# Two batches' attention masks moved to TensorE, and first loads spread over three queues

## The chip, the cores and the metric

The kernel runs on one core of one Trainium2 chip. The metric is the time of one execution in device microseconds (us). Before the change it is 325.88 us, the median of three runs (325.7 to 327.67).

A core has five engines that run their own instruction streams in order and wait for one another through semaphores: PE (TensorE, matrix products and transposes), DVE (VectorE), ACT (ScalarE), POOL (GpSimd) and SP (SyncE, which here only issues DMAs). DMAs can be issued from SP, ACT or POOL. Only those from POOL convert f32 to bf16 on the way in this kernel.

## The reference, cut to what matters

Two stages follow each other. A sparse attention over 8 batches of 8 heads, 576 positions and 64 dimensions; the first four heads see the last 32 positions ("local"), the other four see the earlier positions with the same remainder by 32 ("strided"). Then a feed-forward layer with an ELU.

```
scores = q @ k.T / sqrt(64)
mask_local   = (rel >= 0) & (rel < 32)
mask_strided = (rel >= 0) & (pos[None, :] % 32 == pos[:, None] % 32)
scores = where(masks, scores, -1e9)          # heads 0-3 local, 4-7 strided
attn = exp(scores - max); attn = attn / (sum(attn) + 1e-9)
x = (attn @ v) as [4608, 512]
h = x @ w_in                                 # [4608, 2048]
out = where(h > 0, h, exp(min(h, 0)) - 1) @ w_out
```

Inputs and output are f32.

## The kernel before, in words

**Attention.** A batch has four pairs of heads: two strided (`s0`, `s1`) and two local (`l0`, `l1`). For a strided pair the positions are sorted by remainder into five groups per head, of 126, 126, 108, 108 and 108 keys and queries, so that each group is one small block; the local pairs use six blocks of 128 keys by 96 queries per head. For each pair, PE transposes q and k (`t_q`, `t_k`, L361 strided and L375 local) into one PSUM bank, and ACT or DVE copies that to SBUF (L364, L378). `scores(u)` (L481) makes the scores of unit u = 0 or 1, half of the blocks each, in a pair of PSUM banks (`pair_a` or `pair_b`); ACT takes the exp into bf16 (L501); `mask(u)` (L506) multiplies the probabilities on DVE by a mask of zeros and ones (L516). There is no maximum subtracted. `av(u)` (L520) multiplies with v, which carries a column of ones, so that the sum of each row comes out too; DVE takes its reciprocal (`rden`, L543) and scales (L544) to `x_s` or `x_l`. `x_out` transposes that into `xT` (L571 strided, L584 local; copies L578, L580 and L588). `halo` (L421) copies the last 32 rows of each local v block to the next block; `v_in` (L414) copies the strided v from `v_raw` to `v_str`. From batch 3 on, other forms of the scores are used (L443), with the masks still on DVE.

**Feed-forward.** 4608 tokens are nine chunks of 512. For each chunk and each of 16 slices m of the hidden layer, PE adds four matmuls of 512 columns (L622), ACT takes the exp (L648), DVE forms min(e, 1) - 1 (L655) and the maximum with h (L657). In chunk 0, the slices in ON_SCALAR take another way: ACT does a Relu as well (L651) and DVE one instruction (L652). The output product is L667, copied by ACT (L671) and stored by SP.

**Order.** Each engine's order is written out by hand. OPENING (L45) lists the steps of batch 0, with fill matmuls on data that nobody reads (L712, `fill.n`) and the first twelve matmuls of chunk 0 (`moe.c`, for c the slice of xT); `S0`, `S1` are batch 1's strided pairs. After it, the attention of batch n+1 is put between the matmuls of chunk n by a table of starts and pitches (TIMES).

**Loads.** `load_strided` (L167) issues five DMAs for one tensor of a batch: one for each head (108 rows of 320 elements) and one for the remaining 18 rows. Batch 0's q goes over SP as f32 into `q_stage`, and is cast by ACT (first pair) and DVE (second pair) at L348. All else goes over POOL and is converted on the way, in this order: strided k, local q, local k, strided v, local v, then batch 1 mixed with `w_in` (L302 to L327). Ahead of them POOL makes the identity and the index ramps from which DVE builds the masks (L263 to L298).

Of the kernel before, what the change touches and what calls it, by code (L numbers as in the profile page):

```python
# [10 lines left out]
F32 = mybir.dt.float32  # L11
BF16 = mybir.dt.bfloat16
I32 = mybir.dt.int32
# [40 lines left out]
ON_SCALAR = (4, 7, 10, 13, 15)  # L54
# [4 lines left out]
def kernel(  # L59
# [74 lines left out]
    mask_w = consts.tile([128, 2 * 126 + 3 * 108], BF16, tag="mask_w")  # L134
    mask_s, mask_s3 = mask_w[:, 0:252], mask_w[:, 252:576]
# [27 lines left out]
    WHOLE = 3  # L163
    raw = {}
# [69 lines left out]
    def clear_nat(i, engine=nc.vector):  # L234

        for name in "kq":
            t = nat[name, "str"][i].rearrange("p (h x) -> p h x", h=4)
            engine.memset(t[96:128], 0.0)
# [6 lines left out]
    def clear_v(i, engine=nc.vector):  # L245
# [8 lines left out]
             for n in "q"}  # L254
    load_strided(0, "q", nc.sync)
# [14 lines left out]
    rel_i = p_k.tile([128, LB], I32, tag="rel_i")  # L270
    nc.gpsimd.iota(rel_i, pattern=[[1, LB]], base=32, channel_multiplier=-1)
# [3 lines left out]
    nc.tensor.transpose(key_ps[0:126, 0:126], key_q[0:126, :], identity[0:126, 0:126])  # L275
    diff = p_k.tile([128, 126], F32, tag="diff")
# [13 lines left out]
    rel = p_k.tile([128, LB], F32, tag="rel")  # L290
    above = p_k.tile([128, LB], F32, tag="above")
    nc.vector.tensor_copy(rel, rel_i)
# [37 lines left out]
    class Pair:  # L330
# [150 lines left out]
        def scores(self, u):  # L481
# [4 lines left out]
            blocks = self.blocks(u)  # L486
            for p, blk, bank, i, nk, nq in blocks:
                at, half = self.place(p, blk)
                d = slice(64 * half, 64 * half + 64)
                kind = "str" if self.strided else "loc"  # L490
                c = 0 if self.strided else LB * blk

                nc.tensor.matmul(sc[:, bank, i * nq:(i + 1) * nq],  # L493
                                 lhsT=kT[kind][self.b % 2][d, at, c:c + 128],
                                 rhs=qT[kind][self.b % 2][d, at, c:c + nq],
                                 start=True, stop=True)
# [6 lines left out]
            if self.b:  # L503
                self.mask(u)
# [45 lines left out]
        def step(self, what):  # L550
# [3 lines left out]
            elif what[1:].isdigit():  # L554
                {"s": self.scores, "m": self.mask, "a": self.av}[what[0]](int(what[1:]))
            else:
                getattr(self, {"x": "x_out"}.get(what, what))()
# [388 lines left out]
```

## Time and profile before

| | |
|---|---|
| median of 3 runs | 325.88 us |
| profiled execution | 327.16 us |
| its span | 325.3 us |
| PE busy | 301.5 us (93%) |
| DVE busy | 243.3 us (75%) |
| ACT busy | 177.8 us (55%) |
| POOL busy | 131.4 us (40%) |
| DMA q0 (POOL's): packets, MB | 67632, 18.10 |
| DMA q1 (SP's): packets, MB | 34469, 17.11 |

The profile shows one execution. Its span begins with the first instruction; all times within it are counted from there. Busy shares are means over the whole span, so they do not say which engine holds up which part. In rows of instructions "x" is the number of them, the first figures are start and length in us, and what stands in brackets is the idle time ahead and what ended it. PE lengths include a latency that neighbours overlap, so that rates are read from the distance of starts. A few per cent of the matmul records are missing (558 of 576 of the output product are there).

### The profile page before, as it was taken

The page shows a single profiled execution, that of the slowest core. Times are in us where ns is not written, and L with a number is a line of the kernel's source. Part 1 is how long each engine was busy: PE and PEld are TensorE (multiplying, and loading weights), DVE is VectorE, ACT ScalarE, POOL GpSimd, SP SyncE. Part 2 cuts the span into 40 slices and gives each one's busy share as a digit, 9 for nine tenths or more (in the row PEclk, how much of TensorE's full clock was granted, in tenths as well). Part 3 has the DMA queues.
Part 4 walks back from the last instruction along what each step waited for, and adds up shares of the span by engine and source line. Part 5 has one row for each costly group of instructions (what it writes and reads, how often), then busy time and mean ns, then how long its engine had stood idle before and what let it go on. Part 6 is the DMA issues. An engine that isn't in the chain of part 4 may idle for free.

```text
span 325.3 us, 6088 instructions
## 1 busy us (share of the span) xinstructions
PE 301.5 (93%) x2205; PEld 150.8 (46%) x2246; DVE 243.3 (75%) x539; ACT 177.8 (55%) x337; POOL 131.4 (40%) x208
## 2 busy tenths in 40 slices
PE   2697888999999999999999999999999999999992
PEld 1463544555544554444444454454445444444440
DVE  6576887787888788988798879887887666866600
ACT  3577885776455664555555655555565444434320
POOL 9579825958389368839823830000000000000000
PEclk9999999999999999999999999999999999999998
DMA  6999999999999999999988992920210001100012
GB/s 112 154 169 120 168 207 139 148 130 162 158 141 97 106 154 172 139 182 169 148 117 143 148 135 62 153 83 35 55 48 32 33 34 54 43 35 33 32 67 72
DMA packets 102138, 35.67 MB, mean 110 GB/s; under 512 B 79885, under 2 KB 97493, under 8 KB 102101
## 3 DMA queue, kind: packets, MB, share of 16 engines
q0 software_dynamic: 67632, 18.10, 64.6%
q1 hardware_dynamic: 34469, 17.11, 24.8%
q8 instruction: 19, 0.31, 0.4%
q14 instruction: 18, 0.15, 0.2%
HBM read 36.70 MB, written 9.44 MB: 142 GB/s over the span
## 4 chain that ended last, share of the span: by engine, by line
PE 86%; DVE 4%; DMA 3%; ACT 3%; issue 2%; POOL 2%; ACTq 0%; POOLq 0%
PE single L667 38%; PE half L622 28%; PE single L622 9%; PE single L535 3%; DMA k_loc<-in_k_dram 3%; PE pair_a L456 2%; PE single L375 2%; PE single L571 1%; ACT e_sb L648 1%; PE pair_a L493 1%; DVE g_sb L657 1%; POOL k_str L178 1%; DVE x_l L544 1%; DVE x_s L544 1%; DVE g_sb L652 1%
## 5 line engine op out<-in xcount | busy, mean ns | idle before, releaser
L667 PE MATMUL single<-w_out_sb,g_sb 128*128 128x512 bf16 x558 | 143.6, 379 | 1.4 <-DVE g_sb L657 0.4
L622 PE MATMUL half<-xT,w_in_sb 128*128 128x512 bf16 x419 | 110.3, 379 | 1.1 <-issue 0.3
L648 ACT ACTIVATE e_sb<-half 128x512 f32<-128x512 f32 x109 | 65.3, 599 | 68.7 <-PE half L622 62.4
L655 DVE TENSOR_SCALAR e_sb<-e_sb 128x512 bf16<-128x512 f32 x139 | 62.0, 446 | 36.5 <-ACT e_sb L648 35.4
L667 PEld LDWEIGHTS <-g_sb 128*128 128x128 bf16 x576 | 53.5, 98 | 59.6 <-DVE g_sb L657 1.2
L622 PEld LDWEIGHTS <-w_in_sb 128*128 128x128 bf16 x576 | 51.7, 98 | 55.2 <-issue 0.2
L657 DVE TENSOR_TENSOR g_sb<-e_sb,half 128x512 bf16<-128x512 bf16 x104 | 71.5, 688 | 3.6
L622 PE MATMUL single<-xT,w_in_sb 128*128 128x512 bf16 x136 | 36.0, 379 | 0.3 <-issue 0.2
L648 ACT ACTIVATE e_sb<-single 128x512 f32<-128x512 f32 x35 | 21.1, 602 | 21.6 <-PE single L622 19.6
L671 ACT COPY o_sb<-single 128x512 f32<-128x512 f32 x36 | 21.1, 586 | 17.7 <-PE single L667 16.5
L535 PEld LDWEIGHTS <-pr 128*128 128x128 bf16 (+3 forms) x352 | 20.9, 105 | 15.0 <-issue 1.1
L178 POOL DMA_DIRECT2D v_raw<-in_v_dram x32 | 19.9, 659 | 15.8 <-DVE v_str L414 15.7
L462 ACT ACTIVATE pr<-pair_a 126x936 bf16<-126x936 f32 (+1 forms) x20 | 19.2, 962 | 11.8 <-PE single L456 11.8
L657 DVE TENSOR_TENSOR g_sb<-e_sb,single 128x512 bf16<-128x512 bf16 x35 | 24.1, 688 | 1.2
L178 POOL DMA_DIRECT2D k_str<-in_k_dram x32 | 20.1, 647 | 7.6 <-issue 3.6
L178 POOL DMA_DIRECT2D q_str<-in_q_dram x28 | 17.6, 651 | 6.3 <-DMA w_out_sb<-in_moe_w_out_dram 2.0
L544 DVE TENSOR_TENSOR x_l<-single,rden 96x384 bf16<-96x384 f32 x32 | 17.7, 554 | 1.1
L501 ACT ACTIVATE pr<-pair_a 128x576 bf16<-128x576 f32 (+2 forms) x20 | 13.1, 653 | 6.9 <-PE pair_a L493 6.9
L544 DVE TENSOR_TENSOR x_s<-single,rden 126x256 bf16<-126x256 f32 (+1 forms) x32 | 15.7, 491 | 1.1
L543 DVE RECIPROCAL rden<-single 96x6 f32<-96x6 f32 (+2 forms) x64 | 11.9, 185 | 3.6 <-PE single L535 3.2
L201 POOL DMA_DIRECT2D q_loc<-in_q_dram x16 | 12.3, 794 | 3.2 <-DMA k_str<-in_k_dram 1.6
L182 POOL DMA_DIRECT2D k_str<-in_k_dram x8 | 4.8, 606 | 19.4 <-PE single L375 6.3
(114 smaller groups left out, 269.0 us busy)
## 6 DMA issues: line engine op xcount, KB each, us to landing
out_dram<-o_sb SPq DMA_DIRECT2D x36, 256.0 KB, 2.2
v_loc<-in_v_dram POOLq DMA_DIRECT2D x8, 288.0 KB, 9.7
k_str<-in_k_dram POOLq DMA_DIRECT2D x32, 67.5 KB, 4.6
v_raw<-in_v_dram POOLq DMA_DIRECT2D x32, 67.5 KB, 4.4
w_in_sb<-in_moe_w_in_dram POOLq DMA_DIRECT2D x4, 512.0 KB, 9.2
w_out_sb<-in_moe_w_out_dram POOLq DMA_DIRECT2D x4, 512.0 KB, 16.7
q_str<-in_q_dram POOLq DMA_DIRECT2D x28, 67.5 KB, 6.9
q_loc<-in_q_dram POOLq DMA_DIRECT2D x4, 288.0 KB, 5.4
```

Of the source, the lines that this page charges most:

```text
L178: engine.dma_start(out=t[0:108, h].rearrange("p g d -> p (g d)"), in_=rows[h, :, 0:30, :].rearrange("t (r g) d -> t r (g d)", g=5))
L201: nc.gpsimd.dma_start(out=t[:, h // 2, 0:4, h % 2], in_=src[name][b, h, 0:512].rearrange("(i p) d -> p i d", p=128))
L462: nc.scalar.activation(both, sc[0:nk, :, 0:w], ACT.Exp, scale=scale)
L501: nc.scalar.activation(halves, sc[0:nk, :, 0:w], ACT.Exp, scale=scale)
L535: nc.tensor.matmul(av[0:m, p, blk - b0, :], lhsT=pr[0:nk, o:o + m], rhs=vt[0:nk, 2 * self.hp + p, blk, :], start=True, stop=True)
L544: nc.vector.tensor_tensor(self.x[0:nq, b0:b0 + n].rearrange("q g p d -> q p g d"), av[0:nq, :, 0:n, 0:D], r.unsqueeze(3).to_broadcast([nq, ...
L622: nc.tensor.matmul(hps, lhsT=w_in_sb[:, c, m * 128:(m + 1) * 128], rhs=xT[:, c, nb * N_TILE:(nb + 1) * N_TILE], start=start, stop=stop)
L648: nc.scalar.activation(e_sb, hps, ACT.Exp)
L655: nc.vector.tensor_scalar(e1_sb, e_sb, scalar1=1.0, scalar2=1.0, op0=ALU.min, op1=ALU.subtract)
L657: nc.vector.tensor_tensor(g_of[nb][:, m, :], e1_sb, hps, op=ALU.max)
L667: nc.tensor.matmul(ops, lhsT=g_of[nb][:, m, kk * 128:(kk + 1) * 128], rhs=w_out_sb[:, m, :], start=(m == 0), stop=(m == MC - 1))
L671: nc.scalar.copy(o_sb, ops)
```

## The change

The masks of batches 0 and 1 are no longer multiplied on DVE. Two new constant tiles, `far_l` and `far_s`, hold 0 where the mask is one and -1e30 where it is zero. For these batches `scores(u)` first issues one matmul per PSUM bank that copies them in (identity as the stationary operand), and the score matmuls add to it, so that the exp gives zero there. OPENING loses its eight mask steps, and its end is put in another order. The halo copy of batch 0 goes from ACT to DVE and later in the order. ON_SCALAR has three slices instead of five.

Batch 0's q is loaded over SP (heads 0, 1 and the 18 rows) and ACT (heads 2, 3), and its strided v too, as f32 into a stage of its own. Strided k and local q and k are issued on POOL before the masks are built; the identity is made on DVE from an index ramp, and one memset goes from POOL to DVE.

```diff
 OPENING = """
-s0.cast_q s0.t_q s0.t_k s1.cast_q s1.t_k s0.s0 s0.m0 s1.t_q s0.s1 s0.m1 fill.2 l0.t_q s1.s1
-s1.m1 s1.s0 s1.m0 l0.t_k l1.t_q fill.1 s0.v l0.s0 l0.m0 l1.t_k l0.s1 s1.a0 s0.a0 l0.m1 l1.s0
-s1.a1 s0.a1 fill.1 l1.s1 l1.m0 fill.1 s1.halo s1.x fill.1 s0.x l1.m1 fill.1 l0.a0 fill.1 l0.a1
-l1.a0 moe.2 l1.a1 S0.t_q l0.x S1.t_q moe.3 l1.x moe.0 moe.1
+s0.cast_q s0.t_q s0.t_k s1.cast_q s1.t_k s0.s0 s1.t_q s0.s1 fill.2 l0.t_q s1.s1
+s1.s0 l0.t_k l1.t_q fill.1 s0.v l0.s0 l1.t_k l0.s1 s1.a0 s0.a0 l1.s0
+s1.a1 s0.a1 fill.1 l1.s1 fill.1 s1.x fill.1 s0.x s1.halo fill.1 l0.a0 fill.1 l0.a1
+l1.a0 moe.2 l0.x l1.a1 S0.t_q moe.3 l1.x S1.t_q moe.0 moe.1
 """.split()
...
-ON_SCALAR = (4, 7, 10, 13, 15)
+ON_SCALAR = (7, 11, 15)
...
+    far_l = consts.tile([128, 3 * LB], BF16, tag="far_l")
+    far_s = consts.tile([128, 126], BF16, tag="far_s")
...
+    FAR = 2
...
-             for n in "q"}
-    load_strided(0, "q", nc.sync)
+             for n in "qv"}
+    raw[0] = stage["v"]
+    load_strided(0, "q", nc.sync, range(2))
+    load_strided(0, "q", nc.scalar, range(2, 4))
+    load_strided(0, "v", nc.sync, range(2))
+    load_strided(0, "v", nc.scalar, range(2, 4))
...
-    clear_nat(0)
-    for i in range(2):
-        nc.vector.memset(kT["str"][i][:, :, 126:128], 0.0)
-    make_identity(nc, identity)
-    nc.gpsimd.memset(mask_w[96:128, 252:576], 0.0)
+    clear_nat(0, names="k")
+    rel_i = p_k.tile([128, 128], I32, tag="rel_i")
+    nc.gpsimd.iota(rel_i, pattern=[[1, 128]], base=STRIDE, channel_multiplier=-1)
...
-    rel_i = p_k.tile([128, LB], I32, tag="rel_i")
-    nc.gpsimd.iota(rel_i, pattern=[[1, LB]], base=32, channel_multiplier=-1)
+    load_strided(0, "k")
+    load_local(0, "q")
+    load_local(0, "k")
+    rel = p_k.tile([128, 128], F32, tag="rel")
+    nc.vector.tensor_copy(rel, rel_i)
+    nc.vector.tensor_scalar(identity, rel, scalar1=float(STRIDE), scalar2=None,
+                            op0=ALU.is_equal)
...
+    clear_nat(0, names="q")
+    for i in range(2):
+        nc.vector.memset(kT["str"][i][:, :, 126:128], 0.0)
+    nc.vector.memset(mask_w[96:128, 252:576], 0.0)
...
+    nc.vector.tensor_scalar(far_s[0:126], mask_s[0:126, 0:126], scalar1=1.0,
+                            scalar2=-NEG, op0=ALU.subtract, op1=ALU.mult)
...
+    nc.vector.tensor_scalar(far_l, mask_l[:, 0:3 * LB], scalar1=1.0, scalar2=-NEG,
+                            op0=ALU.subtract, op1=ALU.mult)
...
-    load_strided(0, "k")
-    load_local(0, "q")
-    load_local(0, "k")
-    load_strided(0, "v")
...
-                copy = nc.vector.tensor_copy if self.b else nc.scalar.copy
-                copy(t[0:32, :, 1:6, 0:D], t[96:128, :, 0:5, 0:D])
+                nc.vector.tensor_copy(t[0:32, :, 1:6, 0:D], t[96:128, :, 0:5, 0:D])
...
+            far = self.b < FAR
+            if far:
+                k, n = blocks[0][4:]
+                g = len(blocks) // 2
+                if self.strided:
+                    t = far_s[0:k, 0:n].unsqueeze(1).to_broadcast([k, g, n])
+                elif u == 0:
+                    t = far_l
+                else:
+                    t = far_l[:, n:2 * n].unsqueeze(1).to_broadcast([k, g, n])
+                for bank in range(2):
+                    nc.tensor.matmul(sc[:, bank, 0:g * n], lhsT=identity[0:k, :],
+                                     rhs=t, start=True, stop=False)
...
-                                 start=True, stop=True)
+                                 start=not far,
+                                 stop=not far or i == len(blocks) // 2 - 1)
...
-            if self.b:
+            if not far:
                 self.mask(u)
```

More of the change, by code (lines that the diff above doesn't have):

```diff
@@ L231, in rows_of, with clear_nat @@
         return t[0:126, h, 0:2, :], t[0:108, h, 2:5, :]
-    def clear_nat(i, engine=nc.vector):
-        for name in "kq":
+    def clear_nat(i, engine=nc.vector, names="kq"):
+        for name in names:
             t = nat[name, "str"][i].rearrange("p (h x) -> p h x", h=4)
@@ L288 @@
                               mask_s[0:108, 0:108])
+    nc.vector.tensor_scalar(far_s[0:126], mask_s[0:126, 0:126], scalar1=1.0,
+                            scalar2=-NEG, op0=ALU.subtract, op1=ALU.mult)
     ml = mask_l.rearrange("p (b j) -> p b j", j=LB)
-    rel = p_k.tile([128, LB], F32, tag="rel")
+    rel = rel[:, 0:LB]
     above = p_k.tile([128, LB], F32, tag="above")
-    nc.vector.tensor_copy(rel, rel_i)
     nc.vector.tensor_scalar(above, rel, scalar1=0.0, scalar2=None, op0=ALU.is_ge)
@@ L554, in step @@
             elif what[1:].isdigit():
-                {"s": self.scores, "m": self.mask, "a": self.av}[what[0]](int(what[1:]))
+                {"s": self.scores, "a": self.av}[what[0]](int(what[1:]))
             else:
```

## The prediction, made before the result

> **What bounds the kernel now.** I read the page's share rows, then busy time by stretch, the chain of waits, the PE timeline, and the waits of the stretch that is not full.
>
> ```profile
> PE   2697888999999999999999999999999999999992
> DMA  6999999999999999999988992920210001100012
> ...
> 6.40:14.70 8.30, 5.86 (x54) 3.12 (x54) 4.93 (x15) 3.85 (x7) 5.45 (x8) 1.00 1.36 163
> 14.70:22.90 8.20, 7.31 (x99) 5.52 (x102) 5.33 (x16) 6.29 (x11) 5.56 (x10) 1.00 1.62 165
> 22.90:28.50 5.60, 4.90 (x57) 3.07 (x56) 3.20 (x9) 2.68 (x7) 4.88 (x9) 1.00 0.95 111
> 28.50:55.00 26.50, 21.19 (x225) 11.79 (x228) 23.10 (x51) 21.76 (x41) 15.18 (x23) 1.00 1.35 175
> ...
> 60.00:150.00 90.00, 89.05 (x732) 45.19 (x745) 76.81 (x166) 53.32 (x103) 63.37 (x100) 1.00 1.47 146
> ```
>
> The last rows are start:end and length, then busy PE, weight loads, DVE, ACT, POOL. From 55 us on PE is full. It can lose or save time only in the opening (to 28.5 us) and in batch 1's attention (28.5 to 55), where DVE has the most work (23.10 of 26.50) and PE is idle 5.3. Whatever these 55 us give is passed on unchanged to the end.
>
> ```profile
> 2.35 1.31 POOL k_str L178 x2
> ...
> 6.07 8.65 DMA k_loc<-in_k_dram
> 14.71 0.04 issue
> 14.76 0.71 PE single L375 x12
> ...
> 22.80 0.35 PE single L535 x6
> ...
> 25.49 0.56 DVE x_l L544
> ```
>
> The opening's chain (start, length): POOL issues loads from 2.35, `k_loc` lands at 14.71, then PE works in order to 22.80, then DVE normalises the last local rows to 26.05.
>
> ```profile
> 10.89 1.04 PE L712 MATMUL single<-mask_l,identity 128*128 128x512 bf16 x2
> 22.16 0.63 PE L712 MATMUL single<-mask_l,identity 128*128 128x512 bf16 x1
> 22.96 0.38 PE L712 MATMUL single<-mask_l,identity 128*128 128x512 bf16 x1
> ```
>
> The same fill matmul shows PE's rate: 0.63 us until 22.2, 0.38 from 23.0. Two in a row take 1.04, so 0.40 apart (0.78 ns a column); L622's four in 1.04 later are 0.215 apart (0.42 ns). PE reaches its full rate only at about 23 us.
>
> **The change part by part.** The profiled execution took 327.16 us (span 325.3 and 1.9 around it), 1.28 over the median of 325.88; I sum against 327.16 and carry the difference to the median.
>
> *Masks on PE.* A strided pair's units have 504 and 648 columns in two matmuls each, a local pair's 576 twice: 4.6 thousand columns for a batch of eight units. That is 3.6 us at the first rate, 1.95 at the second, for each of two batches. The first 0.39 hides behind ACT's copy of `kT`; 0.71 and 0.83 us of idle PE ahead of `q_loc` and `k_loc` can cover the other strided ones (1.4), if those loads are not later. The four local units of batch 0 (1.8) stand on the chain.
>
> *Masks off DVE.* L516 ran eight times for each batch: 411 to 497 ns, 3.6 us a batch. In batch 0 DVE was idle beside them, but the stretch from the first `rden` (18.23) to the last `x_l` (26.05) held three of them (1.27) and 1.26 of waiting for PE. In batch 1 DVE is the busiest engine.
>
> *Fewer units on ACT's Relu (five to three, m = 11 new).* DVE gains 0.43 (L655) plus 0.69 (L657) less 0.69 (L652) twice, +0.9; ACT loses two of 0.59 (L651). Batch 1's DVE: 3.6 less, 0.9 more, net 2.7 less. PE has 1.95 more.
>
> *Halo of batch 0 to DVE.* ACT's 1.26 us at 21.16 becomes DVE's 0.49 (batch 1's row), placed after the strided rows, where DVE waited 1.26. Cost nothing; 0.5 if PE gets so fast that the wait is gone.
>
> *Setup.* POOL loses the identity's memset and select (0.20, 0.29) and one memset (0.36) ahead of `k_str`; its next bound is DVE's clearing of `k_str`, done at 1.66. So `k_str`, `q_loc`, `k_loc` are issued about 0.6 sooner. DVE gains the identity, `far_s`, `far_l` and a memset: no row has these forms; between L293 (0.21, 96 columns) and L655 (0.43, 512 columns) I take 0.25 each, 0.1 for the memset, less some empty waits. Its setup ends near 9.1 instead of 8.5, and queued behind it is the copy of `qT` (8.42), which the first scores need: +0.7.
>
> *First loads.* ACT issues four DMAs (q heads 2, 3, v heads 2, 3), SP six. SP's took 0.5 to 1.0 us each, so ACT's table load (1.28) moves from 0.75 to about 4.2 and `rden`'s fill ends near 6.0, beside the wait for q: free. The q loads alone are seen here:
>
> ```profile
> q1 hardware_dynamic: 131, 0.16, 49.3%
> ...
> q0 software_dynamic: 235, 0.06, 63.2%
> q1 hardware_dynamic: 118, 0.14, 43.0%
> ```
>
> These are packets, MB and share of 16 engines in 3 to 4 us (SP's queue nearly alone) and in 6 to 7 (with POOL's). Alone, one such queue keeps 49% busy. The trace has 45 packets of four bytes on it, completion writes, nine for each of the five DMAs: they say that a load of 18 x 6 rows uses nine engines. So 131 packets in a microsecond on nine engines is 69 ns each: they were nearly full with q alone. q's 549 packets are about 3.7 us of those nine; v, now there too, another 3.7; and `k_str`, `q_loc`, `k_loc` share the same engines. ACT's second half of q competes with SP's first half, which ACT's first cast awaits: landing at 5.9 becomes 5.9 to 8, I take 7.2. `k_loc` (14.71): 0.6 sooner at best, by v's 3.7 less 0.6 and less some gaps (2.5) later at worst; I take 16.2.
>
> The Trainium skill, DMA: Bandwidth & Descriptors (Issuing engines are not separate DMA queues), says that DMAs of the three issuing engines run on the same 16 engines and interleave, so that more queues save only issue time; by that rule v's f32 work is added in front, as in the worst end above. The trace agrees in that q's packets fell from 131 to 118 a microsecond beside POOL's.
>
> POOL has five DMAs fewer ahead of `v_loc`; `w_in` and batch 1's loads, issued at 12.88 and from 15.34, come some 3 us sooner, behind `k_loc` on the same queue. No PE wait hung on them; I count nothing. v's conversion on DVE now reads f32: two copies at 0.35 become at most 0.7 each (L348's f32 casts: 0.36 for half the columns), but its wait of 1.51 for `v_raw` goes; nothing is counted.
>
> *Order.* Between the last `x_l` (26.05) and `l1.x` (27.19) PE ran `S1.t_q` (0.43) and `moe.3` (0.65); now `moe.3` comes before that `l1.x` and `S1.t_q` behind it. Gain 0.6, between 0 and 1.1.
>
> *The sum.* First scores at 10.5 instead of 9.55 (`q` and setup). PE would be ready for `k_loc` at 14.76 + 0.95 + 1.4 - 1.5 = 15.6; the load at 16.2 decides, +1.45. Then 8.04 us of PE to 22.80, plus 1.8 of masks. With more long matmuls in a row the full rate should come sooner; I take 19.6, halfway between 16.1, the end of the first local transposes, and 23. Then 3.4 us run at the first rate, and the 6.4 left shrink to about 4.2, since ACT's four exps (0.65) and DVE's eight pieces hold them: `l0.a0` at 23.8, +1.0. Order -0.6: the opening +0.4. Batch 1: PE's floor is 21.2 plus some 0.9 of lost records plus 1.95, 24.1. What PE waits for there:
>
> ```profile
> PE pair_a L493 <- ACT pr L501: 1.4, 4, 0.7
> PE single L571 <- DVE x_s L544: 1.2, 2, 0.7
> PE single L584 <- DVE x_l L544: 0.8, 1, 0.8
> ```
>
> DVE's 2.0 should go almost wholly with 2.7 less work ahead of them, ACT's stay in part (next late: the exp of the one `pair_a`). I take 24.9 instead of 26.5, -1.6. Together -1.2: 326.0 for the profiled execution, **324.7** for the median.
>
> **Rivals.**
>
> *Faster: the masks warm PE early, and the local loads are hardly later.* The strided masks and the two fills put about 2.6 us of long matmuls between 10 and 13.4, as many as in an equal stretch before 23. If the full rate comes by 13 to 16, the eight microseconds after `k_loc` are cut to what DVE needs, its chain 2.0 shorter without masks and waits. Opening -2.7, batch 1 -1.8: -4.5, **321.4**. For it: PE worked without a break from 14.76 to 23 at half rate. Against it: the gap ahead of `q_loc`. The Trainium skill, TensorE: Matmul & The Clock Gate (Part 1), gives a free-running window of about 3.4 us of activity before the full rate, and in Part 4 says that transposes do not count as activity; the trace agrees that transposes from 6.4 on had not raised the rate by 22. By that rule the phase of the window decides between this case and mine.
>
> *Slower: v jams the nine engines.* q at 8 (+2), `k_loc` past 17.2 (+2.5), the rate no sooner than 23, so all 1.8 of local masks at 0.78 ns: +4.3, less 0.6 of order; batch 1 gains nothing, as PE's 1.95 eats what DVE gives. With some 0.3 of idle more, +4.0: **329.9**. It decides from `k_loc` at about 17 on. For it: 43 and 63% at once in 6 to 7, and the chain's 8.65 us. Against it: the engines above nine had slack early.
>
> *It cancels.* DVE was not what held batch 1; PE's extra work fills exactly its idle time: **325.9**.
>
> **Chances.** Forecast 0.38, faster rival 0.34, slower 0.22, cancelled 0.06. A measurement of this kernel tells about 1% (3.3 us) from no change. Faster by more 0.34, within 0.44, slower 0.22. The range takes most of both rivals: **320.5 to 329.5**.
>
> **What would show it.** Right: `k_loc` lands at 15.5 to 17; the first cast starts near 7; a fill of 0.38 before 20; no L516 before 60; PE idle in the 26 us after the opening under 3.5; the first L648 near 28.9; DVE there near 20.4. Wrong: locals on time and 0.38 by 16 (faster rival), or 0.63 still at 22 and `k_loc` past 17 (slower one), or PE idle in batch 1 as before, where the masks' wait for `pair_a` would be the new bound.

## The result, and the profile after

The changed kernel takes **331.70 us** (median of six runs, 329.58 to 333.30); the kernel before, beside it on the same chip, 326.84 (six runs, 325.70 to 327.67). The ratio is **1.0135**, 95% interval 1.0096 to 1.0174: 1.35% slower, and above the predicted range (320.5 to 329.5). The profiled execution of the changed kernel took 329.58 us (span 327.8), the lowest of its six, against 327.16 (325.3) for the one of before. The pair of traces therefore shows 2.4 of the 4.9 us that the medians show.

The page of the changed kernel, PE's and the DMA engines' slices:

```profile
PE   0598898999999999999999999999999999999993
DMA  5999999999999999989998991930110000100012
```

A slice is 8.2 us here. The first one, in which PE was a fifth busy or more before, is empty: PE's first batch starts later.

Busy time by stretch of the changed kernel (start:end, length, then busy PE, weight loads, DVE, ACT, POOL, granted clock, DMA share, GB/s):

```profile
6.40:14.70 8.30, 3.08 (x21) 1.61 (x21) 3.50 (x15) 1.65 (x4) 4.68 (x8) 1.00 1.45 209
14.70:22.90 8.20, 8.12 (x128) 4.51 (x125) 2.66 (x8) 6.47 (x11) 3.35 (x6) 1.00 1.58 167
28.50:55.00 26.50, 23.53 (x250) 12.64 (x247) 18.36 (x40) 21.15 (x39) 14.61 (x22) 1.00 1.33 173
```

PE did 3.08 us of work between 6.4 and 14.7 instead of 5.86. In batch 1 DVE fell from 23.10 to 18.36, as the masks left it; PE rose from 21.19 to 23.53, by 2.34. Two things go into these differences. The stretch is fixed and batch 1 runs later in the changed kernel: over the same work, 30.1 to 57.7 us, DVE is busy 20.5 and PE 23.4. And the trace of before lacks five matmul records there, an estimated 1.1 us at 0.215 each. The granted clock reads 1.00 in all these rows only because the profile's records of it begin with the full rate (at 17.09 here); that PE ran at half rate before is seen in the lengths of its matmuls.

The chain of waits of the changed kernel, at its start (start, length):

```profile
3.92 0.52 POOL k_str L182
4.43 9.09 DMA k_str<-in_k_dram
13.57 0.50 PE single L374 x3
```

The transfer on the chain is now the strided k, whose last load was issued at 4.43 and landed at 13.53 (before: 9.04), not `k_loc`, which landed at 15.84 (before: 14.71).

PE's timeline of the changed kernel (start, length, then the idle time ahead and its releaser in brackets; L374 is L361 of before, L388 is L375, L738 is L712):

```profile
9.63 1.01 PE L374 MATMUL single<-identity,q_str 126*128 126x126 bf16 x5 [6.90 <-ACT q_str L361]
11.15 0.68 PE L374 MATMUL single<-identity,k_str 126*128 126x126 bf16 x5 [0.51 <-DMA k_str<-in_k_dram]
12.74 0.39 PE L374 MATMUL single<-identity,k_str 126*128 126x126 bf16 x2 [0.91 <-DMA k_str<-in_k_dram]
13.57 0.50 PE L374 MATMUL single<-identity,k_str 126*128 126x126 bf16 x3 [0.44 <-DMA k_str<-in_k_dram]
...
16.31 0.97 PE L738 MATMUL single<-mask_l,identity 128*128 128x512 bf16 x2
17.21 0.45 PE L388 MATMUL single<-identity,q_loc 96*64 96x96 bf16 x12
18.76 0.45 PE L388 MATMUL single<-identity,k_loc 96*64 96x96 bf16 x12
19.39 0.39 PE L738 MATMUL single<-mask_l,identity 128*128 128x512 bf16 x1
```

Before, the q transposes began at 6.39 and those of the second pair's strided k at 8.91. Now q's begin at 9.63, the second pair's k at 12.74, and the last three of them at 13.57. `q_loc` and `k_loc` are met without a wait. The full rate comes at 17.1 (from the granted clock; the transposes at 17.21 take 0.45 where they took 0.69), six microseconds sooner than before.

To follow the time I compare the starts of the same feed-forward matmul in two profiles, read from its weight load, of which no record is missing: the seventh of L622 (27.2 us in the profile of before, "opening"), the 65th (56.0, "after batch 1"), and PE's last matmul ("end"). In the changed kernel they are 1.6, 2.7 and 3.05 us later. So 1.6 are lost in the opening in spite of the early full rate, another 1.1 in batch 1 and 0.35 later. Behind PE's last matmul the copies and stores win back 0.55, so that the span is 2.5 longer.

### The profile page after: what moved, and what is told of

Its sections match the earlier page's. It is cut to its first block, busy times and chain, and to the rows that moved or that the text cites. A ratio compares the mean times of both kernels' runs of the same rounds, so it can differ in the third digit from the quotient of the medians.

```text
span 327.8 us, 6182 instructions
## 1 busy us (share of the span) xinstructions
PE 306.0 (93%) x2278; PEld 150.2 (46%) x2278; DVE 238.7 (73%) x530; ACT 176.2 (54%) x334; POOL 127.6 (39%) x200
## 3 DMA queue, kind: packets, MB, share of 16 engines
HBM read 36.70 MB, written 9.44 MB: 141 GB/s over the span
## 4 chain that ended last, share of the span: by engine, by line
PE 85%; DVE 6%; DMA 3%; ACT 3%; issue 1%; POOL 1%; ACTq 0%
PE single L693 37%; PE half L648 28%; PE single L648 8%; PE single L561 3%; DMA k_str<-in_k_dram 3%; DVE g_sb L683 2%; PE pair_a L468 2%; PE single L388 1%; PE single L597 1%; DVE e_sb L681 1%; PE pair_a L518 1%; ACT e_sb L674 1%; PE single L374 1%; DVE x_l L570 1%; DVE x_s L570 1%
## 5 line engine op out<-in xcount | busy, mean ns | idle before, releaser
L693 PE MATMUL single<-w_out_sb,g_sb 128*128 128x512 bf16 x576 | 146.0, 379 | 0.4 <-DVE g_sb L683 0.4
L648 PE MATMUL half<-xT,w_in_sb 128*128 128x512 bf16 x436 | 112.5, 380 | 0.0
L681 DVE TENSOR_SCALAR e_sb<-e_sb 128x512 bf16<-128x512 f32 x141 | 62.8, 445 | 40.9 <-ACT e_sb L674 40.1
L683 DVE TENSOR_TENSOR g_sb<-e_sb,half 128x512 bf16<-128x512 bf16 x106 | 72.9, 688 | 3.7
L561 PEld LDWEIGHTS <-pr 128*128 128x128 bf16 (+3 forms) x352 | 20.1, 102 | 14.2 <-issue 0.6
L182 POOL DMA_DIRECT2D v_raw<-in_v_dram x28 | 17.7, 688 | 17.5 <-DVE v_str L427 16.7
L182 POOL DMA_DIRECT2D k_str<-in_k_dram x32 | 19.6, 631 | 11.0 <-DMA w_out_sb<-in_moe_w_out_dram 3.9
L205 POOL DMA_DIRECT2D k_loc<-in_k_dram x16 | 12.2, 784 | 1.6 <-DMA v_raw<-in_v_dram 1.2
## 6 DMA issues: line engine op xcount, KB each, us to landing
w_out_sb<-in_moe_w_out_dram POOLq DMA_DIRECT2D x4, 512.0 KB, 17.2
```

The source lines that it names most:

```text
L182: engine.dma_start(out=t[0:108, h].rearrange("p g d -> p (g d)"), in_=rows[h, :, 0:30, :].rearrange("t (r g) d -> t r (g d)", g=5))
L205: nc.gpsimd.dma_start(out=t[:, h // 2, 0:4, h % 2], in_=src[name][b, h, 0:512].rearrange("(i p) d -> p i d", p=128))
L561: nc.tensor.matmul(av[0:m, p, blk - b0, :], lhsT=pr[0:nk, o:o + m], rhs=vt[0:nk, 2 * self.hp + p, blk, :], start=True, stop=True)
L648: nc.tensor.matmul(hps, lhsT=w_in_sb[:, c, m * 128:(m + 1) * 128], rhs=xT[:, c, nb * N_TILE:(nb + 1) * N_TILE], start=start, stop=stop)
L681: nc.vector.tensor_scalar(e1_sb, e_sb, scalar1=1.0, scalar2=1.0, op0=ALU.min, op1=ALU.subtract)
L683: nc.vector.tensor_tensor(g_of[nb][:, m, :], e1_sb, hps, op=ALU.max)
```

## The experiments

Each ratio is against the kernel before, run beside the kernel on the same chip. Single runs of one kernel scatter over some 5 us, so the ratios judge, and a profile only tells where one execution lost its time. Shifts are in us against the profile of before, negative for sooner; the third column has the start of the first q transpose on PE and the landings of the last strided k and of batch 0's local k; the last column is the end of the half rate by the granted clock.

| kernel | median | ratio (95%) | q on PE / strided k / local k landed | opening, after batch 1, end | full rate at |
|---|---|---|---|---|---|
| before | 326.84 | 1 | 6.39 / 9.04 / 14.71 | 0, 0, 0 | 22.97 |
| changed | 331.70 | 1.0135 (1.0096 to 1.0174) | 9.63 / 13.53 / 15.84 | +1.6, +2.7, +3.05 | 17.09 |
| loads_alone | 329.68 | 1.0101 (1.0057 to 1.0144) | 9.09 / 13.77 / 16.52 | +1.9, +2.6, +2.6 | 18.02 |
| masks_old_loads | 327.08 | 1.0016 (0.9986 to 1.0045) | 8.09 / 9.98 / 12.90 | -1.75, -0.7, -0.3 | 13.96 |
| v_on_pool | 328.31 | 1.0036 (1.0002 to 1.0071) | 9.18 / 9.69 / 12.51 | -1.6, +0.2, +0.3 | 13.55 |
| all_on_sp | 328.04 | 1.0056 (1.0022 to 1.0091) | 7.53 / 9.74 / 15.17 | -1.6, +0.2, +1.1 | 14.70 |
| q_sp_v_act | 330.65 | 1.0104 (1.0064 to 1.0145) | 9.57 / 12.49 / 15.28 | +1.0, +3.0, +3.0 | 17.16 |
| sixteen_rows | 329.59 | 1.0079 (1.0045 to 1.0112) | 10.58 / 9.56 / 14.58 | 0, +1.0, +1.0 | 15.25 |
| relu_alone | 328.20 | 1.0048 (1.0017 to 1.0080) | 7.37 / 9.43 / 12.99 | -1.4, +0.15, +0.85 | 20.96 |
| relu_as_before | 326.52 | 0.9986 (0.9947 to 1.0025) | 7.88 / 9.54 / 12.55 | -2.45, -1.7, -1.6 | 12.76 |
| changed_relu5 | 328.66 | 1.0054 (1.0016 to 1.0091) | 9.78 / 13.41 / 16.15 | +4.85, +5.2, +5.25 | 26.25, see text |
| batch0_only | 326.93 | 0.9976 (0.9932 to 1.0020) | 8.06 / 10.03 / 12.97 | 0, +1.0, +1.45 | 18.64 |
| old_start_batch0 | 326.97 | 0.9999 (0.9970 to 1.0029) | 6.44 / 9.29 / 12.81 | -2.65, -1.25, -0.8 | 12.83 |
| old_start_both | 327.59 | 1.0013 (0.9981 to 1.0045) | 6.71 / 9.35 / 13.02 | +2.2, +3.4, +3.5 | 25.33 |
| before_heat | 326.81 | 1.0003 (0.9981 to 1.0025) | 6.65 / 9.44 / 12.92 | -2.75, -1.3, -0.3 | 4.59, see text |
| masks_heat | 326.76 | 1.0004 (0.9978 to 1.0030) | 7.14 / 8.82 / 12.81 | -3.0, -1.8, -1.0 | 6.68 |
| changed_heat | 331.08 | 1.0130 (1.0101 to 1.0159) | 9.87 / 12.85 / 16.15 | +1.5, +4.4, +4.4 | 3.88, see text |

How much one profile can differ from the next is seen in `relu_alone`, whose opening is that of before, line for line: its opening is 1.4 us sooner, with local k landed at 12.99 instead of 14.71 and the full rate 2.0 sooner. In the four other profiles with the first loads of before, local k landed at 12.81 to 13.02; the 14.71 of the profile on which the prediction rests was the odd one. Differences of this size in an opening are no evidence for an edit.

The theory after the first comparison: the new first loads make q and the strided k late, and that is the whole loss. Its rival: the masks on PE cost what they save and more.

### Taking the change apart: the loads, and the rest

`loads_alone` is the kernel before with nothing but the new first loads.

```diff
-             for n in "q"}
-    load_strided(0, "q", nc.sync)
+             for n in "qv"}
+    raw[0] = stage["v"]
+    load_strided(0, "q", nc.sync, range(2))
+    load_strided(0, "q", nc.scalar, range(2, 4))
+    load_strided(0, "v", nc.sync, range(2))
+    load_strided(0, "v", nc.scalar, range(2, 4))
...
-    load_strided(0, "v")
```

> The kernel before with the new first loads only (q over SP and ACT, strided v over SP and ACT as f32); masks on DVE as before. Theory A: first cast after 8.5 and the last strided k after 12, and the time 4 to 7 us over the kernel before, 331 to 334, worse than the changed kernel, since PE's early full rate is missing. Theory B: within 1 us of the kernel before.

`masks_old_loads` is the changed kernel without them: q on SP alone, v on POOL behind local k. All else of the change stays.

```diff
-             for n in "qv"}
-    raw[0] = stage["v"]
-    load_strided(0, "q", nc.sync, range(2))
-    load_strided(0, "q", nc.scalar, range(2, 4))
-    load_strided(0, "v", nc.sync, range(2))
-    load_strided(0, "v", nc.scalar, range(2, 4))
+             for n in "q"}
+    load_strided(0, "q", nc.sync)
...
     load_local(0, "k")
+    load_strided(0, "v")
```

> The changed kernel with the first loads as before: q over SP alone, strided v as bf16 over POOL behind local k. Masks on PE, new setup, new order and three Relu slices stay. Theory A (the loads cost the time: in the changed kernel the first cast began at 9.17 instead of 5.93 and the last strided k landed at 13.5): the first cast is back at 6 to 6.5, the last strided k lands before 9, and the time is 2 to 4 us under the kernel before, about 323 to 325. Theory B (the mask matmuls on PE cost it): still 2 us or more over the kernel before, 329 or more.

The loads alone give 1.0101; the rest without them 1.0016. Both are smaller than expected: the loads cost 2.6 us and not 4 to 7, and without them the kernel is no different from before, where 2 to 4 us of gain were expected. PE's timeline of `loads_alone` (L364 is L361 of before) shows the same places as the changed kernel:

```profile
9.09 1.01 PE L364 MATMUL single<-identity,q_str 126*128 126x126 bf16 x5 [6.06 <-ACT q_str L351]
11.27 0.69 PE L364 MATMUL single<-identity,k_str 126*128 126x126 bf16 x5 [1.16 <-DMA k_str<-in_k_dram]
13.21 0.39 PE L364 MATMUL single<-identity,k_str 126*128 126x126 bf16 x2 [1.26 <-DMA k_str<-in_k_dram]
```

There POOL issues the strided k as late as before (from 2.35), so it is not the earlier issue that holds it up; it is what SP and ACT put beside it. The theory stands for half of the 1.35% or more: 1.0 to 1.2% by these two runs, and 0.7% (1.0054 against 0.9986) where five slices keep their Relu, as runs further down show.

### Which part of the loads

Three versions of the changed kernel keep a part of the new loads. In `v_on_pool` q stays split over SP and ACT, and v goes back to POOL. In `all_on_sp` q, then v as f32, go over SP alone. In `q_sp_v_act` q goes over SP and v over ACT.

```diff
 v_on_pool
-    load_strided(0, "v", nc.sync, range(2))
-    load_strided(0, "v", nc.scalar, range(2, 4))
...
     load_local(0, "k")
+    load_strided(0, "v")
 all_on_sp (q_sp_v_act: nc.scalar for v)
-    load_strided(0, "q", nc.sync, range(2))
-    load_strided(0, "q", nc.scalar, range(2, 4))
-    load_strided(0, "v", nc.sync, range(2))
-    load_strided(0, "v", nc.scalar, range(2, 4))
+    load_strided(0, "q", nc.sync)
+    load_strided(0, "v", nc.sync)
```

> The changed kernel with strided v as bf16 over POOL behind local k again; q stays split over SP and ACT. If the amount of f32 on the nine engines is the jam (v's 590 KB there): the first cast at 6.5 to 7.5, the last strided k by 9.5, the time within 1 us of masks_old_loads. If two hardware queues at once are the trouble: the first cast still after 8.5, and the time at most 2 us under the changed kernel.

> The changed kernel with q and then strided v as f32 over SP alone, nothing from ACT. If the nine engines are the jam: the first cast at 6 to 7, since q is ahead in its queue, but the last strided k still after 11, time 327 to 330. If two hardware queues at once are the trouble: strided k by 9.5 as well, and the time within 1 us of masks_old_loads.

> The changed kernel with q all on SP and v (f32) all on ACT. If two hardware queues beside POOL's cost what they do whatever they carry, the first transposes of q start past 9 us, the last strided k past 12.5, and the ratio is 1.010 to 1.014. If the harm is in splitting q, so that one pair waits for a half that stands behind the other queue, q is as with all on SP: first transposes at 7.5 to 8, k at about 10, ratio 1.003 to 1.007.

With v off the hardware queues 1.0036 is left; with the same bytes as in the changed kernel on one hardware queue, 1.0056; on two, with another division, 1.0104. Of the expectations only that of `q_sp_v_act` came in full. In `v_on_pool` the first cast was as late as two queues were to make it (8.73), but the strided k landed as it does without them (9.69; 9.98 in `masks_old_loads`). In `all_on_sp` the nine engines were to hold the strided k past 11, and it landed at 9.74. ACT's first cast of q in the kernel before started at 5.93. In `all_on_sp` and in the changed kernel:

```profile
7.07 0.82 ACT L359 CAST q_str<-q_stage 126x256 bf16<-126x256 f32 x2 [4.42 <-DVE v_loc L252]
```

```profile
9.17 0.82 ACT L361 CAST q_str<-q_stage 126x256 bf16<-126x256 f32 x2 [2.62 <-DVE kT_loc L323]
```

The releasers named there had long been done; the cast waited for the stage. In one queue q stands ahead of v, and its cast starts 2.1 sooner than in the changed kernel. With two, SP's first half of q shares the engines with everything that ACT has issued. In the changed kernel SP's queue moved 85 packets in the half microsecond from 3.5, with ACT's first load done and POOL's not begun, and 12 or 13 in each half between 4.5 and 6, when all three had loads under way; ACT's moved 3, 3 and 12 there. Splitting q is thus not needed for the harm (`q_sp_v_act` doesn't split it), and a second hardware queue without v costs little (`v_on_pool` 1.0036, `masks_old_loads` 1.0016, within the intervals). The full 1% comes where v's f32 bytes go out on a second queue beside q and k. They also start sooner there: v is issued from 3.0 us in the changed kernel and from 0.75 in `q_sp_v_act`, but from 4.85 in `all_on_sp`. Whether the second queue does the harm or v's earlier start, no run here separates.

### Do nine engines make the jam?

The prediction read nine completion writes for each of these loads as nine engines in use. `sixteen_rows` cuts each f32 load of a head into one of 16 x 6 rows and one of 2 x 6.

```diff
+        if engine is not nc.gpsimd:
+            for h in heads:
+                engine.dma_start(out=t[0:96, h]..., in_=rows[h, 0:16, 0:30, :]...)
+            for h in heads:
+                engine.dma_start(out=t[96:108, h]..., in_=rows[h, 16:18, 0:30, :]...)
...
```

> The changed kernel with each f32 load of a head cut into one of 16 x 6 rows and one of 2 x 6 rows, so that the large ones can go over sixteen engines where 18 x 6 rows went over nine (sixteen completion writes for them in place of nine). If the nine engines are the jam, the first cast starts before 7.5, the last strided k is used by 10.5, and the ratio is 1.007 or less. If the queues hinder each other wherever their packets go, or the four more DMAs on each queue cost as much, the first cast stays at 8.5 to 10 and the ratio at 1.010 to 1.016.

The large loads now leave sixteen completion writes each, and those of q's four heads are complete by 4.9 (in the changed kernel the second load of each queue was completed between 6.2 and 7.8). The strided k landed at 9.56 instead of 13.53, and the ratio falls from 1.0135 to 1.0079. That fits nine engines as a part of the jam but does not show it, and neither expected case came as a whole. Issuing more DMAs also moved v's issue, from 3.0 to 4.0 us on ACT and from 3.2 to 5.2 on SP, so that q and k had the engines longer without it. And it brought a new wait: ACT issues four more DMAs, and its table load and the cast stand behind them in order (ACT's timeline of `sixteen_rows`):

```profile
5.90 2.40 ACTq L187 DMA_DIRECT2D v_stage<-in_v_dram  x2
8.32 1.28 ACT L279 ACT_TABLE_LOAD   x1 [8.32 <-DMA v_stage<-in_v_dram]
10.14 0.80 ACT L375 CAST q_str<-q_stage 126x256 bf16<-126x256 f32 x2
```

The cast has no wait ahead of it any more: ACT itself is late, and the strided k, which PE meets at 11.39, is no longer waited for.

### Three slices of Relu instead of five

`relu_alone` is the kernel before with the new ON_SCALAR; `relu_as_before` is `masks_old_loads` with the old one; `changed_relu5` is the changed kernel with the old one.

```diff
 relu_alone
-ON_SCALAR = (4, 7, 10, 13, 15)
+ON_SCALAR = (7, 11, 15)
 relu_as_before, changed_relu5
-ON_SCALAR = (7, 11, 15)
+ON_SCALAR = (4, 7, 10, 13, 15)
```

> The kernel before with three Relu slices (7, 11, 15) instead of five, nothing else. Theory A with the Relu cut as the loss: 0.7 to 1.5 us slower, ratio 1.002 to 1.005, since DVE, with 23.1 of 26.5 us in batch 1, gets 0.9 more. If it costs nothing: ratio within 0.001 of 1.

> masks_old_loads with the five Relu slices of the kernel before; batch 1's masks stay on PE. If the Relu cut is what batch 1 loses (DVE's 0.43 more in each of two slices, just ahead of x_l): about as batch0_only. If PE's added mask matmuls (1.95 us) are: as masks_old_loads, ratio 1.000 to 1.003.

> The changed kernel with five slices with a Relu, as before, in place of three. If the cut costs in batch 1 what it cost alone (1.0048), the ratio is 1.007 to 1.010; if it is free beside the late loads, or pays because DVE no longer has the masks, it is 1.013 or more.

The cut costs 0.5% in the kernel before, 0.3% with the old loads and 0.8% in the changed kernel: the same sign three times, though only the first interval excludes one by itself (the others are differences of two ratios). In the changed kernel it costs more than expected (1.0054 with five slices, where 1.007 to 1.010 stood). The place is the end of batch 1. PE's waits between 40 and 61 us, in `masks_old_loads` (three slices) and in `relu_as_before` (five):

```profile
PE single L607 <- DVE x_l L567: 1.2, 1, 1.2
```

```profile
PE single L607 <- DVE x_l L567: 0.8, 1, 0.8
```

The same in the changed kernel and in `changed_relu5`:

```profile
PE single L610 <- DVE x_l L570: 1.3, 1, 1.3
```

```profile
PE single L610 <- DVE x_l L570: 0.8, 1, 0.8
```

PE waits there for DVE's last `x_l`. In the kernel before with three slices (`relu_alone`) it is 1.3, with five 0.8. So three pairs agree: the cut adds 0.4 to 0.5 to this wait, and with five slices it is 0.8 whether DVE has the 3.6 us of masks or not. That is not the whole cost. From slice to slice the trace of `masks_old_loads` falls 0.46 behind that of `relu_as_before` at slice 6, wins back 0.33 at slice 8 and 0.23 at slice 12, and loses 0.45 at slice 15, 0.34 in all; the ratios differ by 0.3%, about 1 us, and the rest of that is not located.

### The masks themselves

`batch0_only` is `relu_as_before` with the masks of batch 0 alone on PE. `old_start_batch0` and `old_start_both` take the whole setup and the loads of the kernel before, with q, k and v issued where they were, and only the masks (of one batch, of two), the order, the halo on DVE and five slices of Relu.

```diff
 batch0_only, old_start_batch0
-    FAR = 2
+    FAR = 1
 old_start_batch0, old_start_both
+    make_identity(nc, identity)
...
-    load_strided(0, "k")
-    load_local(0, "q")
-    load_local(0, "k")
...
+    load_strided(0, "k")
+    load_local(0, "q")
+    load_local(0, "k")
+    load_strided(0, "v")
```

> masks_old_loads with batch 1's masks back on DVE and the five Relu slices of the kernel before: PE masks in batch 0 alone. In masks_old_loads the opening was 1.75 us ahead of the kernel before at the twelfth feed-forward matmul, and batch 1 gave 1.05 of that back by the 64th. Theory A (batch 1's masks and Relu cut cost batch 1): 1.2 to 2 us under the kernel before, ratio 0.994 to 0.997. Theory B (any gain of the opening is lost in batch 1, since transfers or other waits hold it): ratio 0.999 to 1.002, with the gain gone by the 64th matmul.

> The kernel before with its own setup and first loads (identity on POOL, strided k issued from 2.3), plus PE masks in batch 0 alone, the new order of the opening and the halo on DVE. If the earlier start of strided k is what moved the first cast of masks_old_loads to 7.6 (q's second load was thinned out as soon as POOL's packets came): first cast back at 6, first transposes at 6.4, opening 2.5 to 3.5 us ahead of the kernel before, ratio 0.990 to 0.994. If the first cast is late for another reason: first cast after 7, ratio as batch0_only.

> Setup and first loads as in the kernel before (k, local loads behind the masks on POOL, q on SP alone, v on POOL), the masks of both batches on TensorE, five slices with a Relu, the new order and halo. If the mask matmuls of batch 1 only replace DVE's work there and keep TensorE busy enough for its clock to stay up, there is no half-rate stretch at 30 to 35 us and the ratio is 0.990 to 0.995 (opening about 2.5 us sooner, kept to the end). If batch 1's masks cost TensorE what DVE gives, or the clock falls again for a window, the ratio is 0.998 to 1.002, like the version with batch 0's masks only.

With `relu_as_before` that makes four versions with the masks on PE and none of the harm, at 0.9976 to 1.0013: the masks give nothing that this measurement can tell, for one batch or two. `batch0_only` lies between its two expected cases, and its interval covers both. Of `old_start_batch0` the first half came: with the strided k issued as late as before, the first cast is back at 5.98. Put together, the first cast starts at 5.93 to 6.91 in the five profiles with the old start, at 6.43 to 7.63 in the four with the strided k issued about 0.3 sooner, at 8.73 with q split over two queues as well, and at 9.17 with v too: as far as single profiles tell, each step of bringing loads forward delays q. The second half did not come: the sooner opening is not in the time (0.9999 instead of 0.990 to 0.994). Of the two with the old start, the profile of one begins the feed-forward 2.65 us sooner, that of the other 2.2 us later, though they issue the same opening. Their loads land alike (strided k 9.29 and 9.35, local k 12.81 and 13.02). The difference is the time of the full rate. The fills of `old_start_batch0`, then of `old_start_both` (L733 is L712 of before):

```profile
12.07 0.97 PE L733 MATMUL single<-mask_l,identity 128*128 128x512 bf16 x2
19.17 0.39 PE L733 MATMUL single<-mask_l,identity 128*128 128x512 bf16 x1
```

```profile
12.13 1.03 PE L733 MATMUL single<-mask_l,identity 128*128 128x512 bf16 x2
23.25 0.61 PE L733 MATMUL single<-mask_l,identity 128*128 128x512 bf16 x1
24.14 0.63 PE L733 MATMUL single<-mask_l,identity 128*128 128x512 bf16 x1
25.60 0.38 PE L733 MATMUL single<-mask_l,identity 128*128 128x512 bf16 x1
```

In one the rate is full from 12.8, in the other from 25.3, with the same long matmuls in PE's queue. The profiled execution of the second (330.10) is one of its two slowest of twelve; its median is 327.59.

### Is it the rate of PE at all?

That left open whether the changed kernel loses by waiting or by the idle, cold start that the waiting brings. A constant tile is set at the start, and matmuls on it that nobody reads keep PE busy from 1.1 us to between 5.7 and 7.3: four ahead of the transpose of the key ramp, then 8 in the kernel before (`before_heat`), 11 in `relu_as_before` (`masks_heat`), 14 in the changed kernel (`changed_heat`).

```diff
+    heat = p_k.tile([128, 128], BF16, tag="heat")
+    nc.vector.memset(heat, 1.0)
+    def fill(n):
+        for _ in range(n):
+            nc.tensor.matmul(singles[3], lhsT=heat,
+                             rhs=heat.unsqueeze(1).to_broadcast([128, 4, 128]),
+                             start=True, stop=True)
+    fill(4)
...
     nc.tensor.transpose(key_ps[0:126, 0:126], key_q[0:126, :], identity[0:126, 0:126])
+    fill(8)
```

> The kernel before, with twelve matmuls of 512 columns on a constant tile that nobody reads, four ahead of the transposes of the key ramp and eight ahead of the first transposes of q (1.2 to about 6.3 us, where TensorE stood idle but for one transposes). If TensorE's work from the start brings its full rate sooner, the full rate comes by 12 and the ratio is 0.990 to 0.995; if the time of the full rate does not follow from the work, or the opening then waits for loads and the vector engine instead, the ratio is 0.998 to 1.002.

> The version with q on SP alone, v on POOL, five slices with a Relu and both batches' masks on TensorE, with four and eleven such matmuls ahead of q. Alone that version measured 0.9986. If its single executions differ by when the full rate comes (12.8 us in one profile, 25.3 in that of a like one), an early rate makes all of them like the fast ones: 0.988 to 0.994. If not, 0.997 to 1.002, and the masks on TensorE give nothing at any rate.

> The changed kernel with four and fourteen such matmuls ahead of q. If its loss is the late q and strided k, TensorE has the full rate sooner but still waits for them: first transposes of q past 8.5, last strided k past 12.5, ratio 1.007 to 1.012 (the early rate takes back up to 2 us after 14). If the loss is the late full rate that the idle start brings, the ratio is 1.003 or less.

The rate follows: full at 4.6, 6.7 and 3.9 us. The time does not. The clean case is `masks_heat`, where the rate stays full from there on: six microseconds sooner than in `relu_as_before` (12.76), it is no faster (1.0004 against 0.9986). In `before_heat` the rate falls back from 8.00 to 14.83. PE's timeline of `changed_heat` (L385 is L361 of before):

```profile
9.87 0.23 PE L385 MATMUL single<-identity,q_str 126*128 126x126 bf16 x1 [3.31 <-ACT q_str L372]
...
12.08 0.39 PE L385 MATMUL single<-identity,k_str 126*128 126x126 bf16 x2 [0.79 <-DMA k_str<-in_k_dram]
12.90 0.50 PE L385 MATMUL single<-identity,k_str 126*128 126x126 bf16 x3 [0.42 <-DMA k_str<-in_k_dram]
```

The first transposes are quick (0.23), then PE waits for the same late loads, the rate falls back at 10.7, and the ratio is 1.0130. So this run did not have the full rate where it was wanted: it is back only at 17.53, as in the changed kernel (17.09), and the opening is as late (+1.5 and +1.6). It does not part the two causes. The profile of the changed kernel does: it had the full rate 5.9 us sooner than the one of before and lost 1.6 in the opening all the same, with 6.9 us of waiting for q (3.4 before) and 1.9 for the strided k (0.3). A late rate can come on top: `changed_relu5` has the same opening, and its profiled execution, the slowest of its ten (332.24), got the full rate at 26.25 and its opening was 4.85 late.

`before_heat` says why an earlier opening is worth so little. Its feed-forward starts 2.75 us sooner and ends 0.3 sooner, in an execution at its median (326.85). Not all of the 2.75 is the rate's, since local k landed at 12.92 there (`relu_alone`, without fills, has 1.4). PE's waits of it between 22 and 55 us:

```profile
PE single L546 <- DVE pr L527: 1.5, 1, 1.5
PE single L633 <- DMA w_in_sb<-in_moe_w_in_dram: 1.4, 1, 1.4
```

Neither stands in the list of before: PE now comes to the third quarter of `w_in` before it has landed, and to batch 1's first `av` before DVE has masked. The first costs 1.0 of the lead for good; it goes with the masks on PE. The second is nearly made up behind it, since waits of before fall away there: the lead is 1.6 ahead of it, 0.2 in it and 1.3 behind it. (It is 0.7 in `masks_old_loads`, 1.0 in `relu_as_before` and absent in `masks_heat`.) Of the 1.3 that are left after batch 1, 0.3 go at 67 us and 0.7 at 134, where PE waits 0.4 for DVE's `x_l`.

## Why the prediction was wrong, point by point

- **First loads.** This is the first step that failed. "k_loc (14.71) ... I take 16.2" was near as a landing (15.84) and priced the wrong transfer: PE came to `k_loc` only at 18.76. The strided k was costed at nothing, with its issue counted as 0.6 sooner (it was 0.3), and it landed at 13.53 instead of 9.04: 4.5 us on the chain where the sum had none. The working itself held the ground for it: q and v were 3.7 us each on nine engines, and `k_str` was named among what shares them; the sum then passed the delay to the last load in the queue and not to the first that PE waits for. The opening, put at +0.4, became +1.6 in the profiles; in the medians the loads cost 0.7 to 1.2%.
- **q.** The first cast was put at 7.2 with bounds of 5.9 to 8; it came at 9.17. The bound counted the competition of ACT's half of q. By the runs, the earlier strided k alone takes the cast to 6.43 to 7.63, the split to 8.73, and v to 9.17.
- **The rule on issuing engines.** The rule of the Trainium skill (DMA: Bandwidth & Descriptors, Issuing engines are not separate DMA queues) that more queues save only issue time pointed the right way. The runs go further: the same bytes cost 1.0056 over one hardware queue and 1.0104 to 1.0135 over two, where v also started sooner.
- **Setup.** DVE's setup was to end at 9.1; it ended at 9.18. `far_s` took 0.19, `far_l` 0.35, the identity 0.23, against 0.25 each. Right, and hidden behind the late q.
- **PE's rate.** Taken at 19.6, it came at 17.1. That it came near is luck: the same opening had the full rate at 17.09 in the changed kernel and at 26.25 in `changed_relu5`, and that of the two kernels with the old start at 12.83 and 25.33. What a gain there wins was priced wrongly, too: "Whatever these 55 us give is passed on unchanged to the end" holds for the delay of `loads_alone` (+2.6 after batch 1 and at the end) and not for the gain of `before_heat` (-1.3, then -0.3).
- **Batch 1.** This is the second step that failed, and in the pair of profiles the larger one: "-1.6" became +1.1. DVE's work fell as forecast (from 23.1 to 20.5 over the same work, 2.6 where 2.7 was counted), and PE had the mask matmuls more. But "DVE's 2.0 should go almost wholly" was wrong. PE's waits of the changed kernel in batch 1 (L597 is L571 of before, L610 is L584, L510 the masks ahead of L493):

```profile
PE single L597 <- DVE x_s L570: 1.3, 2, 0.9
PE pair_a L510 <- ACT pr L527: 0.7, 1, 0.7
```

With the 1.3 for `x_l` shown above, DVE's 2.0 became 2.6; of the `x_l` wait 0.5 is the Relu cut's (0.8 in `changed_relu5`). Only the waits for ACT fell, the 1.4 of `pr` to 0.7. The step counted DVE's work as one sum and not by what stands ahead of each wait.
- **Relu.** "+0.9 on DVE" was drowned in the net of 2.7; by itself the cut costs 0.3 to 0.8%.
- **The rivals.** The slower one was the right mechanism, loads that jam one another, at 329.9; its place (`k_loc`) and its conditions (`k_loc` past 17.2, the rate no sooner than 23) were not, and the Relu cut was missing from it. The faster one's early full rate nearly came true (17.1, where it asked for 13 to 16) and did not make the kernel faster.
- **The signs.** Three signs of being right came true although the forecast was wrong: `k_loc` at 15.84, a fill of 0.39 at 19.39, and DVE's 20.5. None of them watched the strided k. The first cast (9.17 for 7) and PE's idle time in batch 1 (4.2 of 27.6 us, for under 3.5) did show it.

What stays open: half of the loss in the medians is not in the pair of profiles, because the profiled execution of the changed kernel was its quickest. That the others got the full rate later, as in `changed_relu5`, would fit; no run here shows it. That they lost it again for a window, as in `changed_heat`, does not fit: 3.41 us at half rate take 0.005 off an execution's mean granted clock, and that is 0.998 to 0.999 in the three slowest of the six (331.89, 332.90, 333.30). (The half rate of the opening is not in this mean, which counts the time ahead of the first record as full: it is 0.997 in the profile of before, with the half rate until 22.97.)

## What to carry to other kernels

When loads are begun sooner over more queues, price the first transfer that an engine waits for, with all that is then in flight beside it, and not the last one in the queue. Work moved between engines is worth what the wait that ends last there becomes, not the difference of the busy sums; and a gain at the start is kept only as far as the next thing that another engine sets, here DVE's masks ahead of the first `av` of batch 1 and later its `x_l`. Part by part, undoing the loads and the Relu cut brought the changed kernel from 1.0135 to 0.9986, no different from the kernel before; nothing tried here was faster than it by more than the measurement tells.

## What the runs showed of the hardware that was not expected

- The rate of PE changes on a grid. In `before_heat` the granted clock is full from 4.59, half from 8.00, full from 14.83; in `changed_heat` 3.88, 10.71, 17.53, and again half from 41.43 to 44.84. The steps are 3.41 us and multiples of it. The Trainium skill, TensorE: Matmul & The Clock Gate (Part 1), gives a free-running window of about 3.4 us; these traces agree with it. The fills of `before_heat` show it in their durations:

```profile
1.10 1.89 PE L262 MATMUL single<-heat 128*128 128x512 bf16 x4 [1.10 <-DVE heat L258]
...
2.99 2.68 PE L262 MATMUL single<-heat 128*128 128x512 bf16 x8
...
11.26 1.04 PE L723 MATMUL single<-mask_l,identity 128*128 128x512 bf16 x2
...
18.00 0.39 PE L723 MATMUL single<-mask_l,identity 128*128 128x512 bf16 x1
```

- That page of the Trainium skill lets a busy window bring the full rate. These traces agree only in part. In all 17 profiles PE was busy at least 2.79 us in the 3.41 ahead of each change to the full rate. But in `old_start_both` it was busy throughout in the windows that end at 15.09 and 21.91, and the full rate came at 25.33; its twin had it at 12.83. What else decides is not shown here.
- The half rate came back for one window in the middle of work, too: 41.43 to 44.84 in `changed_heat`, 29.9 to 33.3 in `old_start_batch0`, 31.2 to 34.6 in `relu_alone`, 32.3 to 35.7 in `batch0_only`. What went ahead is the same each time. With the two falls in the opening (8.00 in `before_heat`, 10.71 in `changed_heat`) there are six, and in the 3.41 us before each PE was busy 0.65 to 1.84 us. In every other window at full rate up to 300 us, in all 17 profiles, it was busy 1.93 or more, and the rate stayed. So in these traces a window with PE busy for little more than half of it costs the next one its rate; none of the four in the middle of work held a gap longer than 1.5 us.
